# Seven block products in the last unit's third pair, routing steps spread anew, expert weights asked for later

## The chip, the cores and the metric

The kernel runs on one core of a Trainium2 chip. What counts is the time of one execution on the device, in microseconds (us). The engines named below are TensorE (PE, matrix products), VectorE (DVE), ScalarE (ACT), GpSimd (POOL) and SyncE (SP, which issues DMAs).

## What is computed

Three layers follow one another, for 4 batches of 576 positions and 512 features: linear attention over 8 heads; a block `u + relu(u @ w_ch1) @ w_ch2` with `u = x + U,V mixing`, hidden width 2048; and a top-1 mixture of 8 experts, hidden width 1024. The part of the reference that the change touches:

```python
    u = x + h.transpose(0, 2, 1)
    ch = np.maximum(u @ w_ch1, 0.0) @ w_ch2
    return u + ch
...
    logits = np.einsum('bsd,de->bse', x, w_gate)
    local_gate = 1.0 / (1.0 + np.exp(-np.einsum('bsd,de->bse', x, w_local).squeeze(-1)))
    for b in range(B):
        prev_e = -1
        for s in range(S):
            fresh_e = int(np.argmax(logits[b, s]))
            if s == 0 or local_gate[b, s] < 0.5:
                e = fresh_e
            else:
                e = prev_e if prev_e >= 0 else fresh_e
            prev_e = e
            ...
            h = np.maximum(x[b, s] @ w1[e], 0.0)
            out[b, s] = p[e] * (h @ w2[e])
```

All is in fp32. The kernel splits each fp32 operand into a high and a low part and does three matmuls for each product (high by high, low by high, high by low), so PE's work is three times what the reference says.

## The kernel before

**Stages.** Attention comes first. Then come 12 items of the feed-forward block: 4 units (g = 0 to 3, a quarter of the hidden width each) by 3 pairs p, where a pair is two blocks of 384 columns (TW). They are items 0 to 11, and unit 3 is items 9, 10 and 11. Then come 8 items of the experts: 4 batches by 2 units, with two blocks of 288 columns (CH), items 12 to 19. Each item has two matrices, so two phases on PE: a first matrix from x (L1168 to L1170) with a relu to h, and a second from h into y. A 2 by 2 by 2 block product takes eight block products; with sums of blocks made beforehand and afterwards it takes seven (the Strassen-Winograd scheme), which is 84 matmuls in place of 96. First matrices use seven in most items (the blocks are A11 to A22 and the sums S1 to S4 of the weights; B11 to B22 and the sums T1 to T4 of the moving side). DVE makes the sums afterwards: u adds, `t1`, `t3` and `t2` (psf<-psf,u), in this order, then the low parts of h (L1131). In the last unit, items 9 and 10 (`ZI`) use seven for the second matrix too (`z_steps`, matmuls on L1168 to L1170 as well); item 11 uses the plain form (`mm2`, L1494 to L1496). For that plain form the fourth weight block V3 is parked in DRAM (`park`, `wd`) and fetched again (`w_back`).

**Order of work.** The program is recorded by hand: generators for the item's steps, and threads for weights ("w") and x ("x"), are advanced side by side, and a model of each engine's time (`free`) decides when a thread goes on. Each engine then works through its own list in order. After each step of an item (13 to 16 of them) `side` runs.

**Routing.** From item 10 on `side` starts `route(b)` for batch b (item 10 + b), eleven stages which choose the expert that the batch uses. `PLANS[b]` gives for each stage the step, counted from that item's step 0 with 16 to an item, at which it is recorded. The stages are: the gate's 16 matmuls, their transposes with a maximum (`lg`, `r_sh`), three stages of small DVE instructions that end with the rows `tr`, five transposes of `tr` on PE (L1605) with six ACT copies (L1609), a scan over the positions on DVE (L1612), a count (L1616), a product (L1619), DMAs, and the maximum over the experts (`r_ix`) that gives the index of the expert.

**Weights of the experts.** `w_moe` loads a unit's weights by DMA on SP into half buffers (`halfraw`: 4 halves of `raw`, and rows as long as more than 5 are free, up to 7), and for each block ACT makes the high part (L379) and DVE subtracts it for the low part (L373). For seven block products `w_seven` also makes the weights' sums. The weights of the first batch are asked for at step 7 of item 11.

Of the kernel before, what the change touches and what calls it, by code (L numbers as in the profile page):

```python
# [7 lines left out]
F32 = mybir.dt.float32  # L8
# [8 lines left out]
B, H, S, D, F = 4, 8, 576, 64, 128  # L17
# [17 lines left out]
ZU, ZI = (3,), (9, 10)  # L35
# [8 lines left out]
def model(ctx, tc, kq, vx, wphi, ident, up, vp, wff, wg, wmoe1, wmoe2, rconst, outT):  # L44
    nc = tc.nc
# [126 lines left out]
    touched = {}  # L172
    threads = []
    force = [False]
# [144 lines left out]
    wd = dram.tile([4, 8, 128, 512], F32, name="wd")  # L319
# [15 lines left out]
    pieces = {}  # L335
# [75 lines left out]
    def park(u, s, f):  # L411
        nc.sync.dma_start(out=wd[u.g, PIECES.index(s)], in_=f[:, :512])
        there.add((u, s))
# [91 lines left out]
    def w_seven(u, get, free_, eng, p, due, flat=False, pre=""):  # L505
# [24 lines left out]
        else:  # L530
# [6 lines left out]
            if pre:  # L537
                while touched.get(id(a21), 0.0) > free["PE"] + 0.3 and not force[0]:
                    yield "wait"
                park(u, ZV["A21"], a21)  # L540
                touched[id(a21)] = max(transfer(256), touched.get(id(a21), 0.0) + 3.0)
# [32 lines left out]
    def w_back(u, due):  # L574

        yield from parked(u, (ZV["A21"],))
        s = ZV["A21"]
        yield from w_end(u, s, pieces.pop((u, s)), nc.gpsimd, rows)

    halfraw, loading = [], []  # L580

    def w_moe(u, due):
# [10 lines left out]
        while len(halfraw) < 7 and len(loading) == 1 and len(rows) > 5:  # L593
            halfraw.append(rows.pop()[:, :512])
# [749 lines left out]
    def z_item(i):  # L1344
        return i in ZI
# [30 lines left out]
    def z_steps(i):  # L1376
# [10 lines left out]
        def product(w, x, name, first):  # L1387
# [10 lines left out]
            if i == ZI[-1] and w[0] == "S":  # L1398
                wfree.append(u.w.pop("z" + w))
# [249 lines left out]
    PLANS = ((3,10,11,12,12,13,17,18,19,20,22), (8, 10, 11, 12, 12, 14, 18, 20, 21, 22, 25), (2, 5, 7, 9, 11, 14, 16, 18, 20, 22, 25), (2, 5, 7, 9, 11, 14, 16, 18, 20, 22, 25))  # L1649
    PLAN_COST = ((0.0, 0.8, 1.2), (1.4, 0.0, 0.6), (0.6, 0.0, 0.0), (0.7, 0.0, 0.0), (0.6, 0.0, 0.0), (0.0, 2.3, 0.6), (1.4, 0.0, 0.0), (0.75, 0.0, 0.0), (0.75, 0.0, 0.0), (0.0, 0.0, 0.0), (1.2, 0.0, 0.0))  # L1650

    def side(i, step, steps):
# [42 lines left out]
        if i == ZI[-1] and step == 8:  # L1695
            spawn("w", i, w_back(u, i))
        if i == nf - 1 and step == 7:
            spawn("w", last[units[4]], w_moe(units[4], last[units[4]]))
# [4 lines left out]
    def work():  # L1703

        for i in range(n):
# [10 lines left out]
            if z_item(i):  # L1716
                for _ in z_steps(i):
                    side(i, step, steps)
                    step += 1
                    yield  # L1720
                wanted[0] -= 4
                if i == ZI[-1]:
                    u = items[i][0]
                    for s in ("A11", "A12", "A22"):
                        u.w[ZV[s]] = u.w.pop("z" + s)
                        u.done.add(ZV[s])
                continue
# [217 lines left out]
```

## Time and profile before

| | |
|---|---|
| median of 3 runs | 759.8 us (759.16 to 761.56) |
| profiled execution | 760.08 us |
| its span | 758.2 us |
| PE busy | 745.3 us (98%) |
| DVE busy | 637.7 us (84%) |
| ACT busy | 351.7 us (46%) |
| POOL busy | 72.5 us (10%) |

The profile's page and the views of the trace come from the one profiled execution. A row's start is in us from the start of the span. A timeline's row gives the start, the length, the engine, line and instruction, the tiles (out<-in), how many instructions it stands for, and in brackets the idle time before it with what ended it. An instruction's length includes the time until its result is written, so the next can start on the same engine a little before its end; the spacing of starts tells what it costs its engine.

### The profile page before, as it was taken

What the parts mean: (1) busy time and instruction counts of PE and PEld (TensorE: products, weight loads), DVE (VectorE), ACT (ScalarE), POOL (GpSimd) and SP (SyncE); (2) the same over time, 40 slices, a digit from 0 to 9 for tenths busy, and PEclk for the clock granted to TensorE, in tenths of its full rate; (3) what the DMA queues carried; (4) which work ended last, traced back from release to release, by engine and by line L of the source; (5) the groups of instructions that cost most, each with busy time, mean ns of one, the idle gap of its engine ahead of it and who ended that gap; (6) DMA issues with size and microseconds to landing.
All of it is one profiled execution on the core that took longest, in us unless ns stands there. A gap on an engine that the chain in (4) does not pass through costs nothing. (4 is left out here: it accounts for less than half of the span.)

```text
span 758.2 us, 18724 instructions
## 1 busy us (share of the span) xinstructions
PE 745.3 (98%) x7656; PEld 724.1 (96%) x7656; DVE 637.7 (84%) x1277; ACT 351.7 (46%) x769; POOL 72.5 (10%) x116
## 2 busy tenths in 40 slices
PE   7999999999999999999999999999999999999997
PEld 5899898999999999999999999999999999999997
DVE  6889899777569999999799485879877899999975
ACT  5677777665152343313223133343545455555450
POOL 0212233111110000100101001010000000000000
PEclk9999999999999999999999999999999999999999
DMA  6444755324468897950469004482363144243421
GB/s 203 151 132 126 260 183 189 111 80 154 181 242 328 302 332 284 346 171 29 166 241 339 18 1 157 153 287 84 114 210 101 32 125 143 68 136 108 136 69 65
DMA packets 52728, 124.27 MB, mean 164 GB/s; under 512 B 5472, under 2 KB 29152, under 8 KB 52640
## 3 DMA queue, kind: packets, MB, share of 16 engines
q1 hardware_dynamic: 43024, 87.20, 34.1%
q0 software_dynamic: 6160, 32.39, 12.3%
q10 hardware_dynamic: 3456, 3.46, 1.3%
q8 instruction: 61, 1.00, 0.5%
q14 instruction: 27, 0.22, 0.1%
HBM read 88.81 MB, written 34.23 MB: 162 GB/s over the span
## 5 line engine op out<-in xcount | busy, mean ns | idle before, releaser
L1169 PE MATMUL psf<-x,w 128*128 128x384 f32 (+1 forms) x576 | 184.1, 320 | 0.6 <-POOL x L76 0.6
L1168 PE MATMUL psf<-x,w 128*128 128x384 f32 (+1 forms) x576 | 184.4, 320 | 0.0
L1170 PE MATMUL psf<-x,w 128*128 128x384 f32 (+1 forms) x576 | 183.9, 319 | 0.0
L1494 PE MATMUL psf<-h,w 128*128 128x384 f32 (+1 forms) x576 | 182.8, 317 | 0.0
L1495 PE MATMUL psf<-h,w 128*128 128x384 f32 (+1 forms) x576 | 182.3, 316 | 0.0
L1496 PE MATMUL psf<-h,w 128*128 128x384 f32 (+1 forms) x576 | 182.2, 316 | 0.0
L1146 ACT ACTIVATE h<-psf 128x384 fp32r<-128x384 f32 (+1 forms) x144 | 62.9, 457 | 106.7 <-DVE psf L1129 77.7
L1168 PEld LDWEIGHTS psf<-x,w 128*128 128x128 f32 x576 | 108.3, 188 | 1.4 <-issue 1.4
L1169 PEld LDWEIGHTS psf<-x,w 128*128 128x128 f32 x576 | 108.2, 188 | 1.0 <-POOL x L76 0.9
L1494 PEld LDWEIGHTS psf<-h,w 128*128 128x128 f32 x576 | 108.1, 188 | 0.5 <-issue 0.5
L1170 PEld LDWEIGHTS psf<-x,w 128*128 128x128 f32 x576 | 108.2, 188 | 0.0
L1495 PEld LDWEIGHTS psf<-h,w 128*128 128x128 f32 x576 | 108.1, 188 | 0.0
L1496 PEld LDWEIGHTS psf<-h,w 128*128 128x128 f32 x576 | 108.1, 188 | 0.0
L1129 DVE TENSOR_TENSOR y<-psf,y 128x384 f32<-128x384 f32 (+1 forms) x132 | 69.1, 530 | 24.9 <-PE psf L1496 21.3
L1131 DVE SCALAR_TENSOR_TENSOR h<-psf,h 128x384 fp32r<-128x384 f32 (+1 forms) x148 | 69.0, 508 | 21.5 <-ACT h L1146 20.9
L379 ACT CAST w<-row 128x512 fp32r<-128x512 f32 x79 | 46.7, 620 | 53.9 <-DVE row L373 31.8
L373 DVE TENSOR_TENSOR w<-row,w 128x512 fp32r<-128x512 f32 x79 | 52.9, 687 | 10.6 <-ACT w L379 10.6
L857 DVE TENSOR_REDUCE mx<-pj 128x6 f32<-128x768 f32 (+2 forms) x49 | 45.8, 935 | 6.8 <-PE pj L854 6.7
L858 DVE TENSOR_TENSOR pg<-pj,mx 128x768 f32<-128x768 f32 (+2 forms) x49 | 46.1, 941 | 2.5
L887 PE MATMUL kv<-vt,ek 128*64 128x65 f32 (+1 forms) x1152 | 47.1, 230 | 0.8 <-DMA vt<-in_vx 0.8
L756 POOL DMA_DIRECT2D x<-xd x41 | 22.0, 535 | 269.4 <-PE psf L1170 232.5
L1129 DVE TENSOR_TENSOR u<-psf,p 128x384 f32<-128x384 f32 (+1 forms) x64 | 32.4, 513 | 15.3 <-PE psf L1170 14.2
(136 smaller groups left out, 1126.7 us busy)
## 6 DMA issues: line engine op xcount, KB each, us to landing
x<-xd POOLq DMA_DIRECT2D x41, 768.0 KB, 6.9
raw<-in_wff SPq DMA_DIRECT2D x32, 512.0 KB, 3.6
xd<-x SPq DMA_DIRECT2D x21, 768.0 KB, 4.9
raw<-in_wmoe SPq DMA_DIRECT2D x35, 256.0 KB, 3.4
kq<-in_kq SPq DMA_DIRECT2D x14, 576.0 KB, 4.5
row<-in_wmoe SPq DMA_DIRECT2D x29, 256.0 KB, 4.0
vt<-in_vx SPq DMA_DIRECT2D x16, 325.0 KB, 3.0
ud<-y SPq DMA_DIRECT2D x4, 1152.0 KB, 6.6
```

What stands on the lines that cost most here:

```text
L373: eng.tensor_tensor(out=out, in0=a, in1=b, op=op)
L379: nc.scalar.copy(out=w[:, 0], in_=f[:, :512])
L887: nc.tensor.matmul(out[c], lhsT=e[:, half, i, c], rhs=rhs, start=(tl == 0 and half == 0), stop=(tl == 8 and half == 1), skip_group_check=True)
L1129: nc.vector.tensor_tensor(**kw)
L1131: nc.vector.scalar_tensor_tensor(op1=op1, **kw)
L1146: hat[t, f] = act(lambda: nc.scalar.activation(out=hhi, in_=src, func=ACTF.Relu), n_, ready)
L1168: nc.tensor.matmul(ps, lhsT=w[:, 0, c], rhs=x[:, 0, k, :n_], start=(first and k == 0), stop=False, skip_group_check=True)
L1169: nc.tensor.matmul(ps, lhsT=w[:, 0, c], rhs=x[:, 1, k, :n_], start=False, stop=False, skip_group_check=True)
L1170: nc.tensor.matmul(ps, lhsT=w[:, 1, c], rhs=x[:, 0, k, :n_], start=False, stop=(stop and k == 1), skip_group_check=True)
L1494: nc.tensor.matmul(ps, lhsT=wh, rhs=hhi, start=(k == 0), stop=False)
L1495: nc.tensor.matmul(ps, lhsT=wl, rhs=hhi, start=False, stop=False)
L1496: nc.tensor.matmul(ps, lhsT=wh, rhs=hlo, start=False, stop=(k == 3))
```

## The change

Item 11 uses seven block products for its second matrix, as items 9 and 10 do (`z_item` is true for all of unit 3). So parking V3, `w_back` and renaming the weights for `mm2` go, and `wd` has two units in place of four. The weights of the first batch's expert are asked for at step 9 of item 11, not 7. `PLANS[0]` and `PLANS[1]` have other steps. The `w_moe` loop that gives rows to the half buffers tests `len(loading) <= 1` where it tested `== 1`; the list has been appended to just before, so it has one entry at the first call either way. As item 11 holds rows for its second matrix, five half buffers come about, not seven (raw's four and one row).

```diff
-ZU, ZI = (3,), (9, 10)
+ZU = (3,)
...
-    wd = dram.tile([4, 8, 128, 512], F32, name="wd")
+    wd = dram.tile([2, 8, 128, 512], F32, name="wd")
...
-            if pre:
-                while touched.get(id(a21), 0.0) > free["PE"] + 0.3 and not force[0]:
-                    yield "wait"
-                park(u, ZV["A21"], a21)
-                touched[id(a21)] = max(transfer(256), touched.get(id(a21), 0.0) + 3.0)
...
-    def w_back(u, due):
-
-        yield from parked(u, (ZV["A21"],))
-        s = ZV["A21"]
-        yield from w_end(u, s, pieces.pop((u, s)), nc.gpsimd, rows)
-
...
-        while len(halfraw) < 7 and len(loading) == 1 and len(rows) > 5:
+        while len(halfraw) < 7 and len(loading) <= 1 and len(rows) > 5:
...
     def z_item(i):
-        return i in ZI
+        return items[i][0].kind == "ffn" and items[i][0].g in ZU
...
-            if i == ZI[-1] and w[0] == "S":
+            if last[u] == i:
                 wfree.append(u.w.pop("z" + w))
...
-    PLANS = ((3,10,11,12,12,13,17,18,19,20,22), (8, 10, 11, 12, 12, 14, 18, 20, 21, 22, 25), (2, 5, 7, 9, 11, 14, 16, 18, 20, 22, 25), (2, 5, 7, 9, 11, 14, 16, 18, 20, 22, 25))
+    PLANS = ((3, 10, 12, 16, 17, 18, 19, 20, 20, 21, 24), (10, 17, 18, 19, 20, 21, 22, 24, 26, 27, 30), (2, 5, 7, 9, 11, 14, 16, 18, 20, 22, 25), (2, 5, 7, 9, 11, 14, 16, 18, 20, 22, 25))
...
-        if i == ZI[-1] and step == 8:
-            spawn("w", i, w_back(u, i))
-        if i == nf - 1 and step == 7:
+        if i == nf - 1 and step == 9:
             spawn("w", last[units[4]], w_moe(units[4], last[units[4]]))
...
-                if i == ZI[-1]:
-                    u = items[i][0]
-                    for s in ("A11", "A12", "A22"):
-                        u.w[ZV[s]] = u.w.pop("z" + s)
-                        u.done.add(ZV[s])
                 continue
```

What the instructions' order makes of it is shown at three places. In the new program the same lines have smaller numbers by 11 (L1129 is L1118, L1612 is L1601, L1494 is L1483).

On DVE in the first phase of item 11, before, from the end of batch 0's third small stage (`tr`) to the first t1 add (psf<-psf,u; x2 is two in a row, u are the sums of products, p is a copy of the first product, y the running result):

```order
L1129 TENSOR_TENSOR y<-psf,y 128x384 x2
L373 TENSOR_TENSOR w_100<-row_90,w_100 128x512
L1129 TENSOR_TENSOR u_3712<-psf,u_3711 128x384 x2
L1129 TENSOR_TENSOR y<-y,u_3711 128x2x384
L1129 TENSOR_TENSOR y<-y,u_3712 128x2x384 x2
L1612 SCALAR_TENSOR_TENSOR row_89<-row_85,row_89 8x576
L1129 TENSOR_TENSOR u_3711<-psf,p_3710 128x384 x2
L1616 TENSOR_REDUCE r_cnt<-row_89 8x1
L1619 TENSOR_TENSOR row_84<-row_84,row_89 8x576
L1129 TENSOR_TENSOR u_3712<-psf,p_3710 128x384
L1129 TENSOR_TENSOR psf<-psf,u_3712 128x384
```

The same place after:

```order
L1583 TENSOR_TENSOR tr<-r_ex,r_sm 128x5x8
L1118 TENSOR_TENSOR u_3711<-psf,p_3710 128x384 x2
L1118 TENSOR_TENSOR y<-y,u_3712 128x2x384 x2
L76 TENSOR_TENSOR x_106<-y,x_106 128x2x288
L1601 SCALAR_TENSOR_TENSOR row_90<-row_89,row_90 8x576
L1118 TENSOR_TENSOR u_3712<-psf,p_3710 128x384 x2
L1118 TENSOR_TENSOR h_96<-row_84,h_96 128x768
L1605 TENSOR_REDUCE r_cnt<-row_90 8x1
L1608 TENSOR_TENSOR row_85<-row_85,row_90 8x576
L1118 TENSOR_TENSOR psf<-psf,u_3712 128x384 x2
L1118 TENSOR_TENSOR psf<-u_3712,psf 128x384 x2
```

The second u adds, the low part of h_96, and the pair of t1 adds stand behind the scan now, and behind an x subtract (L76); two more x subtracts and the third and fourth of the small stages, which stood in item 10, are recorded just ahead of this piece.

On DVE in front of and in item 12, before, where batch 1's `tr` is done in item 11 and the next rows are weights (w<-row, w<-raw), y adds, and low parts of h:

```order
L1129 TENSOR_TENSOR y<-psf,y 128x384
L373 TENSOR_TENSOR w_3693<-row_84,w_3693 128x512
L373 TENSOR_TENSOR w_104<-row_89,w_104 128x512
L373 TENSOR_TENSOR w_99<-row_85,w_99 128x512
L1129 TENSOR_TENSOR y<-psf,y 128x384
L373 TENSOR_TENSOR w_102<-raw_92,w_102 128x512
L1129 TENSOR_TENSOR y<-psf,y 128x384
L1131 SCALAR_TENSOR_TENSOR h_97<-psf,h_97 128x288 x2
L76 TENSOR_TENSOR x_3703<-y,x_3703 128x2x288
L1131 SCALAR_TENSOR_TENSOR h_95<-psf,h_95 128x288
```

After, the last small stage of batch 1 (L1580 to L1583, which makes `tr`) stands among the low parts of item 12's h:

```order
L1578 COPY tr<-r_fr 128x5x8
L373 TENSOR_TENSOR w_104<-row_87,w_104 128x512
L1120 SCALAR_TENSOR_TENSOR h_97<-psf,h_97 128x288
L1580 TENSOR_REDUCE r_sm<-r_ex 128x5
L1581 TENSOR_SCALAR r_sm<-r_sm 128x5
L1582 RECIPROCAL r_sm<-r_sm 128x5
L1583 TENSOR_TENSOR tr<-r_ex,r_sm 128x5x8
L373 TENSOR_TENSOR w_102<-raw_92,w_102 128x512
L1120 SCALAR_TENSOR_TENSOR h_97<-psf,h_97 128x288
L1549 TENSOR_REDUCE lg<-psf 128x27
```

The five transposes on PE that read `tr` have moved with it from the end of item 11 to the middle of item 12's first phase.

On DVE around the t2 adds of item 14 (batch 1, first unit; h are the relu's results, psf_7609 and psf_7616 the last product's banks), before:

```order
L1131 SCALAR_TENSOR_TENSOR h3_97<-psf_7592,h3_97 128x288
L1131 SCALAR_TENSOR_TENSOR h3_97<-psf_7599,h3_97 128x288
L1129 TENSOR_TENSOR psf_7609<-psf_7609,u2_3711 128x288
L1129 TENSOR_TENSOR psf_7616<-psf_7616,u2_3711 128x288
L373 TENSOR_TENSOR raw1_93<-raw1_93,row5_89 128x512
L1131 SCALAR_TENSOR_TENSOR h2_96<-psf_7609,h2_96 128x288
L1131 SCALAR_TENSOR_TENSOR h2_96<-psf_7616,h2_96 128x288
L373 TENSOR_TENSOR w12_3697<-row6_90,w12_3697 128x512
L373 TENSOR_TENSOR w3_101<-raw1_93,w3_101 128x512
```

After, where the last product's banks are psf_7608 and psf_7615:

```order
L1120 SCALAR_TENSOR_TENSOR h2_96<-psf_7588,h2_96 128x288
L1120 SCALAR_TENSOR_TENSOR h2_96<-psf_7595,h2_96 128x288
L1118 TENSOR_TENSOR psf_7608<-psf_7608,u2_3711 128x288
L1118 TENSOR_TENSOR psf_7615<-psf_7615,u2_3711 128x288
L373 TENSOR_TENSOR w3_101<-raw1_93,w3_101 128x512
L373 TENSOR_TENSOR w9_3694<-raw0_92,w9_3694 128x512
L373 TENSOR_TENSOR w12_3697<-raw1_93,w12_3697 128x512
L373 TENSOR_TENSOR row5_89<-raw0_92,row3_87 128x512
L1120 SCALAR_TENSOR_TENSOR h0_94<-psf_7608,h0_94 128x288
```

Behind the two t2 adds stands at once the subtract for the low part of w3_101. PE at the end of the first phase of item 14 and the first matmuls of its second, before:

```order
L1169 MATMUL psf_7616<-x4_3702,w13_3698 128x288
L1170 MATMUL psf_7616<-x4_3702,w13_3698 128x288
L1494 MATMUL psf_7712<-h1_95,w5_103 128x288
L1495 MATMUL psf_7712<-h1_95,w5_103 128x288
L1496 MATMUL psf_7712<-h1_95,w5_103 128x288
L1494 MATMUL psf_7712<-h1_95,w5_103 128x288
L1495 MATMUL psf_7712<-h1_95,w5_103 128x288
L1496 MATMUL psf_7712<-h1_95,w5_103 128x288
L1494 MATMUL psf_7712<-h0_94,w0_98 128x288
```

After:

```order
L1158 MATMUL psf_7615<-x4_3702,w2_100 128x288
L1159 MATMUL psf_7615<-x4_3702,w2_100 128x288
L1483 MATMUL psf_7710<-h1_95,w10_3695 128x288
L1484 MATMUL psf_7710<-h1_95,w10_3695 128x288
L1485 MATMUL psf_7710<-h1_95,w10_3695 128x288
L1483 MATMUL psf_7710<-h1_95,w10_3695 128x288
L1484 MATMUL psf_7710<-h1_95,w10_3695 128x288
L1485 MATMUL psf_7710<-h1_95,w10_3695 128x288
L1483 MATMUL psf_7710<-h3_97,w3_101 128x288
```

The weight that the seventh to twelfth matmul of the second matrix read was w0_98 and is w3_101. In item 16 the same stands: the subtract for w4_102 follows the two t2 adds.

## Rows read from the trace of the kernel before

**Rows 1.** The page: busy us, share of the span and instructions of PE.

```profile
PE 745.3 (98%) x7656; PEld 724.1 (96%) x7656; DVE 637.7 (84%) x1277; ACT 351.7 (46%) x769; POOL 72.5 (10%) x116
```

**Rows 2.** Waits of PE, 455 to 600 us: us in total, times, longest.

```profile
PE psf L1168 <- DVE y L1129: 0.3, 1, 0.3
```

**Rows 3.** Windows: length, busy us (instructions) by engine, clock, DMA share, GB/s.

```profile
460.17:474.73 14.56, 14.56 (x86) 14.56 (x85) 8.95 (x16) 5.13 (x9) 3.18 (x6) 1.00 0.70 229
474.73:489.48 14.75, 14.75 (x85) 14.55 (x85) 13.92 (x26) 5.25 (x9) 0.53 (x1) 1.00 0.40 149
...
610.83:621.94 11.11, 11.11 (x86) 11.11 (x85) 10.92 (x24) 6.07 (x14) 0.99 (x2) 1.00 0.59 174
...
658.27:669.38 11.11, 11.11 (x86) 11.11 (x85) 10.66 (x24) 5.22 (x13) 0.00 (x0) 1.00 0.63 192
```

**Rows 4.** Timeline of PE, item 10's end: start, length, instruction, idle before and releaser.

```profile
518.43 0.34 PE L1170 MATMUL psf<-h,w 128*128 128x384 f32 x1
519.03 0.41 PE L1168 MATMUL psf<-h,w 128*128 128x384 f32 x1 [0.26 <-DVE y L1129]
519.28 0.34 PE L1169 MATMUL psf<-h,w 128*128 128x384 f32 x1
```

**Rows 5.** DVE groups in item 10's first phase: busy us, mean ns, idle before.

```profile
L1129 DVE TENSOR_TENSOR u<-psf,p 128x384 f32<-128x384 f32 x4 | 2.2, 558 | 3.5 <-PE psf L1170 3.5
...
L1129 DVE TENSOR_TENSOR psf<-psf,u 128x384 f32<-128x384 f32 x2 | 1.1, 566 | 1.4 <-PE psf L1170 1.4
```

**Rows 6.** Timeline of DVE, first phase of item 11.

```profile
520.12 0.18 DVE L1591 TENSOR_REDUCE r_sm<-r_ex 128x5 f32<-128x40 f32 x1
...
520.88 1.01 DVE L1129 TENSOR_TENSOR y<-psf,y 128x384 f32<-128x384 f32 x2
...
522.41 1.01 DVE L1129 TENSOR_TENSOR u<-psf,u 128x384 f32<-128x384 f32 x2
523.34 2.69 DVE L1129 TENSOR_TENSOR y<-y,u 128x768 f32<-128x768 f32 x3
525.94 1.34 DVE L1612 TENSOR_TENSOR_SCAN row<-row,row 8x576 f32<-8x576 f32 x1
527.21 0.98 DVE L1129 TENSOR_TENSOR u<-psf,p 128x384 f32<-128x384 f32 x2
528.12 0.73 DVE L1616 TENSOR_REDUCE r_cnt<-row 8x1 f32<-8x576 f32 x1
528.78 0.73 DVE L1619 TENSOR_TENSOR row<-row,row 8x576 f32<-8x576 f32 x1
...
532.81 0.75 DVE L76 TENSOR_TENSOR x<-y,x 128x576 fp32r<-128x576 f32 x1
```

**Rows 7.** Timeline of ScalarE (ACT), start of item 11.

```profile
521.61 2.45 ACT L1609 COPY row<-psf 8x256 f32<-8x256 f32 x6 [5.01 <-PE psf L1605]
```

**Rows 8.** Timeline of DVE, item 10: the second half of t1.

```profile
501.40 0.57 DVE L1129 TENSOR_TENSOR psf<-psf,u 128x384 f32<-128x384 f32 x1 [0.47 <-PE psf L1170]
```

**Rows 9.** Timeline of ACT, item 10: what follows that t1.

```profile
502.00 0.49 ACT L1238 ACTIVATE row<-psf 128x384 f32<-128x384 f32 x1 [0.55 <-DVE psf L1129]
502.52 0.84 ACT L1363 CAST h<-row 128x768 fp32r<-128x768 f32 x1
```

**Rows 10.** Timeline of DVE, item 12: two weight subtracts.

```profile
564.18 1.30 DVE L373 TENSOR_TENSOR w<-raw,w 128x512 fp32r<-128x512 f32 x2
```

**Rows 11.** Timeline of DVE, around the start of item 14's second phase.

```profile
620.64 2.34 DVE L1131 SCALAR_TENSOR_TENSOR h<-psf,h 128x288 fp32r<-128x288 f32 x6
622.89 0.82 DVE L1129 TENSOR_TENSOR psf<-psf,u 128x288 f32<-128x288 f32 x2
623.62 0.69 DVE L373 TENSOR_TENSOR raw<-raw,row 128x512 f32<-128x512 f32 x1
```

**Rows 12.** Timeline of PE: the eighth matmul of item 14's second phase.

```profile
622.86 0.29 PE L1495 MATMUL psf<-h,w 128*128 128x288 f32 x1
```

**Rows 13.** Timeline of DVE: the t2 adds of item 16.

```profile
669.60 0.82 DVE L1129 TENSOR_TENSOR psf<-psf,u 128x288 f32<-128x288 f32 x2
```

## Prediction

> **What bounds the kernel now.** I read the page's busy times first. TensorE (PE) is busy 745.3 us of the 758.2 us span, 98% [rows 1]. The granted clock is 1.00, the 2.4 GHz level, in every stretch I read. Next came the waits of PE in the 145 us around the change: one, of 0.3 us [rows 2]. Last came the windows by phase, where PE is busy for all of nearly every phase [rows 3]. So two things alone move the end here: matmuls taken away from PE, and waits given to it. A PE wait anywhere after 480 us moves the end by its full length, since no idle time is left behind it to take it up.
>
> The profiled execution took 760.08 us: 758.2 of span and 1.88 outside. The median of the runs is 759.8, so I sum against 760.08 and take 0.28 off at the end. I call "same" what lies within 0.3% of 759.8, that is 757.5 to 762.1; a measurement of this kernel tells no finer.
>
> **What the change takes off PE.** The second matrix of item 11 (unit 3, third pair) goes from 96 matmuls to 84. A phase of 84 such matmuls takes 14.56 us, so 0.1733 each [rows 3]. Twelve matmuls by 0.1733 is **-2.08 us**. The one PE wait sits in front of the last product of item 10: matmuls stand at 518.43 and 519.03 where 0.17 would do, so 0.43 us [rows 4]. It waits for an add to y that stands behind 0.8 us of routing work on VectorE (DVE). In the new order that add comes ahead of the routing, so **-0.43 us**. The parking and fetching of V3 goes too (two DMAs, a cast, a subtract); its DVE share is one 0.60 us subtract, and as DVE still has idle time in item 10 (below) I price it at nothing on PE. The smaller DRAM buffer and the `<= 1` in `w_moe` cost nothing: the list has one entry there either way. All told PE has 2.5 us less to do; if nothing else happened the run would take 757.6, or **757.3** on the median's scale.
>
> **Item 11's first matrix, new order.** With seven products for the second matrix, DVE must make the combinations of h between the two matrices, and PE's last product of the first matrix (S4) is held until `t1` (the add psf<-psf,u) has read its bank. In item 10, which already works so, DVE came to these adds early: it idled 3.5 us ahead of the u adds and 1.4 us ahead of t1, each time for PE [rows 5]. In item 11 the plan of batch 0's route now puts its stages 3 and 4, its scan, its count and its product into the same stretch, and three x subtracts come ahead of the scan too. Prices from starts that follow one another [rows 6]: route stage 0.76 (520.12 to 520.88), x subtract 0.66 (its 0.75 less the 0.09 by which such starts overlap), wide add to y 0.87 (2.60 for three), pair of u adds 0.93, scan 1.27, count 0.66; the product at the end is like the count. Item 11 starts at about 520.8 (without the wait and without the five transposes, which now come after its third product). DVE is free at 521.0 and does one u add 0.47, two stages 1.5, three x subtracts 2.0, three wide adds 2.6 and the first u pair 0.9: 528.5. The scan then waits for ScalarE's six route copies, 2.45 us [rows 7], which can begin only when the transposes are through at about 527.4: 529.8. Scan 1.27, second u pair 0.9, the low half of B22 0.87 (as a wide add), count and product 1.3: t1 starts at 534.15, not at 531. S4 is due at 533.8 (520.8 + six products of 2.08 + 0.5 for the transposes) and gets its bank at 534.9: **+1.1 us** (0 to 1.3; the lower end if DVE gets through 1 us sooner).
>
> The second matrix then needs the low half of B11 at its second matmul. After the second t1 add the relu follows by 0.60, the cast by another 0.52, and the cast lasts 0.84 [rows 8, 9]: 1.96, then 0.95 for the low half. With t1 at 534.6 that is 537.5, where PE would want it at 537.1: 0.5 us with the restart. T1's low half stands behind more adds in the same queue and costs about as much again. Items 9 and 10 show 0.19 of this already (14.75 for 84 matmuls where 14.56 would do) [rows 3], and since I have no shorter chain, I take **+0.9** (0 to 1.1).
>
> One place for the Trainium skill. Adds with an operand in PSUM follow each other at 0.46 here (522.41 to 523.34 for two) [rows 6]. "Perfetto Trace Analysis", section "Optimizing Scalar/DVE Operations", gives DVE a fixed overhead of about 60 ns on SBUF and 125 ns on PSUM. By it each of these adds would stand 65 ns longer in the queue; the rows show no such difference between u adds and half of a wide SBUF add beyond 0.03, so the rows' spacing is what I sum, and by the page's figure t1 would come about 0.5 us later (eight such adds, an estimate).
>
> **Item 12.** Route 1's transposes move from the end of item 11 into item 12, directly behind the stage that makes `tr`. That work is equal, but three restarts behind short transposes cost about 0.1 each, as the start at 519.03 (0.25 to the next, where 0.17 is the rule) [rows 4]: **+0.3**. In front of the transposes DVE must do, after item 11's tail of three wide adds (2.6) and two u adds (0.9), ten pieces: four stages of 0.8, five low halves of 0.38 (2.34 for six), one weight subtract of 0.65 (1.30 for two) [rows 10, 11]. From 555.3, where the last product of item 11 gives its result, that is 3.5 + 3.2 + 1.9 + 0.65 = 564.6 if it never waits. It does wait for relus, since ScalarE has two weight casts and an exponential in front of one of them: 1.7 us at most, 566.3 to 567. PE wants `tr` at 565.5. I take **+1.1** (0 to 1.6).
>
> **Items 14 and 16.** Here the weights matter. Half buffers for expert weights fall from seven to five, because item 11 still holds rows when they are dealt out, and the load is asked for two steps later. The order shows the effect twice: the low half of the second weight that the second matrix needs is now subtracted directly behind the two t2 adds, and PE reads it in its eighth matmul. In the trace those adds start at 622.89 as a pair, 0.73 in all, and the phase at 621.94; the eighth matmul is at 622.86 [rows 3, 11, 12]. With the subtract (0.69, rows 11) behind them it is ready at 624.35, with 0.05 to hand on; the matmul stalls by about 1.5. The t2 adds are late by six products with h (2.34) in front of them; if DVE came on time they would end at about 622.5 and the stall would be 0.4. I take **+1.1** (0.4 to 1.9). Item 16: the adds start at 669.60, the phase at 669.38 [rows 3, 13]; 669.60 + 0.73 + 0.65 + 0.05 = 671.0 against 670.3 (0.92 into the phase, as in item 14), **+0.8** (0.4 to 1.2). In the order of before the two weights that this phase reads first are subtracted some 25 DVE instructions ahead of the t2 adds, so none of this can be seen in the trace.
>
> **Sum.** -2.08 - 0.43 + 1.1 + 0.9 + 0.3 + 1.1 + 1.1 + 0.8 = +2.8; 760.08 + 2.8 - 0.28 = **762.6 us**. All waits at their upper ends (1.3, 1.1, 0.3, 1.6, 1.9, 1.2) give 764.7; at their lower ends (0.8 in items 14 and 16, 0.3 in item 12) 758.4.
>
> **Rivals.**
> *All waits hidden, faster.* DVE is busy only 84% over the span. If ScalarE's route copies come earlier than I think, so that the scan doesn't wait 1.2 us, t1 is on time, S4 and both second-matrix products start without a gap, and the tail into item 12 is short enough for `tr` to be made in time. With t2 on time too, only the 2.5 us remain: 757.3. It decides at t1: at or before 533.0 in item 11. For it: item 10 does the same work with 6 us of DVE idle. Against: item 11 has over 6 us of extra DVE work in that stretch. The Trainium skill leans this way: "Perfetto Trace Analysis", section "Identifying the Most-Contended Engine", says to optimize the engine with the highest occupancy first. That is PE, and by that rule the saved matmuls come through; the trace agrees on which engine it is, but averages over the stretch where DVE is the tighter one.
> *Items 11 and 12 as summed, weights on time in 14 and 16:* +0.9, 760.7. For it: the two phases are 90 us behind the change, and DVE may reach the t2 adds early there.
> *Items 14 and 16 as summed, items 11 and 12 nearly clean:* -2.5 + 0.3 + 1.9, 759.5.
> *The change doesn't save matmuls:* excluded by the order, which has 12 fewer on PE.
>
> **How the numbers follow.** Waits in both places, 760.8 to 764.7, of which most is above 762.1: 0.55. Weights on time: 0.16. Items 11 and 12 clean: 0.15. All hidden: 0.14. Of the first case I put 0.09 within 762.1, so slower 0.46, same 0.40 (0.09 + 0.16 + 0.15), faster 0.14. The range has to reach to the hidden case, as it and the two middle cases hold 0.45: 757.2 to 764.7.
>
> **What will show it.** Right or wrong, item 11's second phase has 84 matmuls of 384 columns and no add of y waits ahead of 519. A PE wait of about 1 us ahead of S4 of item 11 and two of 0.5 in the next two products show the DVE queue; a wait ahead of the transposes of item 12 shows the plan; a wait of about 1 us at the eighth matmul of the second phases of items 14 and 16, released by a weight subtract, shows the weights. I am wrong if t1 in item 11 starts within 0.3 us of PE's fifth product, or if these two weight subtracts end ahead of the phase's start.

## The result, and the profile after

The changed kernel takes 763.89 us (median of 7 runs, 762.77 to 765.13) where the kernel before takes 759.68 us in the same rounds. The ratio is 1.0055, with a 95% interval of 1.0046 to 1.0064: slower by 4.2 us. The forecast was 762.6 us and slower.

The profiled execution of the changed kernel took 763.36 us, with a span of 761.6. The page's first line, to be held against [rows 1], and PE's waits from 455 us to 600 us and from 600 us to the end (us in total, times, longest), the first of them against [rows 2]:

```profile
PE 745.3 (98%) x7644; PEld 722.2 (95%) x7644; DVE 647.9 (85%) x1290; ACT 354.7 (47%) x775; POOL 71.9 (9%) x116
```
```profile
PE psf L1594 <- DVE tr L1583: 1.1, 1, 1.1
PE psf L1158 <- DVE h L1118: 0.7, 2, 0.4
PE psf L1157 <- DVE psf L1118: 0.5, 1, 0.5
```
```profile
PE psf L1484 <- DVE w L373: 2.2, 2, 1.3
PE psf L1157 <- DVE u L1118: 0.7, 1, 0.7
PE psf L1159 <- DVE w L373: 0.4, 1, 0.4
```

PE has 12 matmuls fewer (7644 for 7656). Its busy time is the same 745.3 us even so, in part because the first matmul after a wait is longer (0.40 us below, where [rows 12] has 0.29). Every PE wait that is new is ended by DVE, which does 10.2 us more work (647.9 for 637.7). One wait of 0.3 us has become eight, of 5.6 us in all. Where these stand shows in the windows by phase (length, busy us and instructions of PE, PEld, DVE, ACT and POOL, clock, DMA share, GB/s). Before, the second phase of item 10, both of item 11, the first of item 12, and the second phases of items 14 and 16 (the first phases of these two are in [rows 3]):

```profile
505.36:521.65 16.29, 16.03 (x95) 15.45 (x95) 15.85 (x43) 6.05 (x12) 0.00 (x0) 1.00 0.20 75
521.65:536.30 14.65, 14.65 (x88) 14.65 (x86) 14.24 (x29) 7.13 (x16) 1.02 (x2) 1.00 0.29 110
536.30:555.32 19.02, 19.02 (x124) 17.98 (x123) 15.56 (x44) 7.30 (x16) 0.00 (x0) 1.00 0.47 153
555.32:569.92 14.60, 14.60 (x121) 13.74 (x119) 9.73 (x21) 9.74 (x23) 1.00 (x2) 1.00 0.67 220
...
621.94:634.58 12.64, 12.64 (x98) 12.64 (x97) 12.50 (x30) 6.75 (x16) 0.00 (x0) 1.00 0.26 79
...
669.38:682.03 12.65, 12.65 (x99) 12.65 (x97) 12.40 (x24) 8.22 (x18) 0.00 (x0) 1.00 0.35 109
```

The same phases after, with the first phases of items 14 and 16:

```profile
504.54:519.87 15.33, 15.33 (x91) 15.09 (x90) 15.15 (x35) 6.63 (x12) 0.00 (x0) 1.00 0.13 51
519.87:535.72 15.85, 15.37 (x90) 14.99 (x90) 14.22 (x30) 7.37 (x15) 1.01 (x2) 1.00 0.27 102
535.72:552.84 17.12, 16.43 (x101) 14.85 (x101) 16.98 (x37) 8.92 (x17) 0.00 (x0) 1.00 0.25 80
552.84:569.68 16.84, 15.78 (x128) 14.72 (x128) 13.48 (x42) 8.59 (x22) 0.00 (x0) 1.00 0.61 206
...
610.54:622.58 12.04, 11.35 (x86) 11.12 (x85) 11.41 (x25) 6.97 (x16) 0.98 (x2) 1.00 0.51 157
622.58:636.84 14.26, 12.91 (x99) 12.68 (x98) 12.02 (x29) 6.69 (x15) 0.00 (x0) 1.00 0.31 100
...
660.53:672.30 11.77, 11.33 (x87) 11.10 (x85) 11.67 (x26) 6.82 (x15) 0.00 (x0) 1.00 0.49 161
672.30:686.11 13.81, 12.91 (x98) 12.68 (x97) 13.15 (x25) 8.20 (x18) 0.00 (x0) 1.00 0.38 119
```

| stretch | before | after | difference |
|---|---|---|---|
| item 10, second phase | 16.29 | 15.33 | -0.96 (five transposes moved on, 0.4 of wait gone) |
| item 11, first phase | 14.65 | 15.85 | +1.20 (the five transposes, a wait) |
| item 11, second phase | 19.02 | 17.12 | -1.90 (12 matmuls and ten transposes less, two waits more) |
| item 12, first phase | 14.60 | 16.84 | +2.24 (ten transposes, a wait) |
| item 14, both phases | 23.75 | 26.30 | +2.55 |
| item 16, both phases | 23.76 | 25.58 | +1.82 |

Up to the end of item 12's first phase the sum is +0.58; the saved matmuls are more than paid back there. Items 14 and 16, which begin 58 and 108 us after item 11's second matrix has ended, cost another 4.37. Items 13, 15, 17, 18 and the first phase of item 19 have their old lengths to within 0.1 us. The six differences come to 4.95. The two profiled executions differ by 3.28 only, since the one of after was 0.8 us quicker ahead of item 9 (459.37 for 460.17) and 0.7 behind item 19's first phase, in work that is the same; the medians differ by 4.2.

In item 11 the chain that holds the last product of the first matrix (S4) is seen in three rows: the scan waits for ScalarE's copies, t1 comes behind it, and PE waits for t1.

```profile
528.52 1.35 DVE L1601 TENSOR_TENSOR_SCAN row<-row,row 8x576 f32<-8x576 f32 x1 [0.74 <-ACT row L1598]
...
532.93 1.01 DVE L1118 TENSOR_TENSOR psf<-psf,u 128x384 f32<-128x384 f32 x2
```
```profile
533.54 0.44 PE L1157 MATMUL psf<-x,w 128*128 128x384 f32 x1 [0.48 <-DVE psf L1118]
```

In item 14 the picture is the one of [rows 11, 12]. The DVE timeline there, then PE's (start, length, instruction, idle time before it with its releaser):

```profile
621.29 2.34 DVE L1120 SCALAR_TENSOR_TENSOR h<-psf,h 128x288 fp32r<-128x288 f32 x6
623.54 0.82 DVE L1118 TENSOR_TENSOR psf<-psf,u 128x288 f32<-128x288 f32 x2
624.27 1.89 DVE L373 TENSOR_TENSOR w<-raw,w 128x512 fp32r<-128x512 f32 x3
```
```profile
625.01 0.40 PE L1484 MATMUL psf<-h,w 128*128 128x288 f32 x1 [1.34 <-DVE w L373]
```

ScalarE casts the high parts of three weights from 614.52 to 616.19. By their order these are the three whose subtracts start at 624.27, so neither the load nor the cast is late:

```profile
614.52 1.67 ACT L379 CAST w<-raw 128x512 fp32r<-128x512 f32 x3
```

### The profile page after: what moved, and what is told of

Its sections match the earlier page's. It is cut to its first block, busy times and chain, and to the rows that moved or that the text cites. A ratio compares the mean times of both kernels' runs of the same rounds, so it can differ in the third digit from the quotient of the medians.

```text
span 761.6 us, 18711 instructions
## 1 busy us (share of the span) xinstructions
PE 745.3 (98%) x7644; PEld 722.2 (95%) x7644; DVE 647.9 (85%) x1290; ACT 354.7 (47%) x775; POOL 71.9 (9%) x116
## 5 line engine op out<-in xcount | busy, mean ns | idle before, releaser
L1159 PE MATMUL psf<-x,w 128*128 128x384 f32 (+1 forms) x576 | 183.9, 319 | 0.4 <-DVE w L373 0.4
L1484 PE MATMUL psf<-h,w 128*128 128x384 f32 (+1 forms) x544 | 171.7, 316 | 2.2 <-DVE w L373 2.2
L1483 PE MATMUL psf<-h,w 128*128 128x384 f32 (+1 forms) x544 | 171.9, 316 | 0.0
L1485 PE MATMUL psf<-h,w 128*128 128x384 f32 (+1 forms) x544 | 171.5, 315 | 0.0
L1159 PEld LDWEIGHTS psf<-x,w 128*128 128x128 f32 x576 | 108.2, 188 | 0.7 <-DVE w L373 0.7
L1484 PEld LDWEIGHTS psf<-h,w 128*128 128x128 f32 x544 | 102.1, 188 | 2.7 <-DVE w L373 2.7
L1135 ACT ACTIVATE h<-psf 128x384 fp32r<-128x384 f32 (+1 forms) x136 | 58.7, 454 | 97.8 <-DVE psf L1118 63.7
L1483 PEld LDWEIGHTS psf<-h,w 128*128 128x128 f32 x544 | 102.1, 188 | 0.1
L1485 PEld LDWEIGHTS psf<-h,w 128*128 128x128 f32 x544 | 102.1, 188 | 0.0
L1118 DVE TENSOR_TENSOR y<-psf,y 128x384 f32<-128x384 f32 (+1 forms) x134 | 69.4, 527 | 24.7 <-PE psf L1485 21.1
L1120 DVE SCALAR_TENSOR_TENSOR h<-psf,h 128x384 fp32r<-128x384 f32 (+1 forms) x142 | 65.8, 505 | 16.9 <-ACT h L1135 16.1
L379 ACT CAST w<-row 128x512 fp32r<-128x512 f32 x62 | 37.0, 619 | 45.8 <-DVE row L373 19.9
L373 DVE TENSOR_TENSOR w<-row,w 128x512 fp32r<-128x512 f32 x62 | 41.8, 685 | 10.8 <-ACT w L379 10.8
L379 ACT CAST w<-raw 128x512 fp32r<-128x512 f32 x60 | 35.9, 622 | 21.7 <-DVE raw L373 14.3
```

The source lines that it names most:

```text
L379: nc.scalar.copy(out=w[:, 0], in_=f[:, :512])
L1118: nc.vector.tensor_tensor(**kw)
L1120: nc.vector.scalar_tensor_tensor(op1=op1, **kw)
L1135: hat[t, f] = act(lambda: nc.scalar.activation(out=hhi, in_=src, func=ACTF.Relu), n_, ready)
L1159: nc.tensor.matmul(ps, lhsT=w[:, 1, c], rhs=x[:, 0, k, :n_], start=False, stop=(stop and k == 1), skip_group_check=True)
L1483: nc.tensor.matmul(ps, lhsT=wh, rhs=hhi, start=(k == 0), stop=False)
```

## The experiments

Theories at the start: (A) the weights are late in items 14 and 16 because five half buffers came about in place of seven; (B) they are late because DVE's queue is full of the second matrix's adds. Each run below is a kernel with the edit that is shown or named; times are medians, and the ratio is to the kernel before in the same round.

**Five half buffers in the kernel before.**

```diff
-        while len(halfraw) < 7 and len(loading) == 1 and len(rows) > 5:
+        while len(halfraw) < 5 and len(loading) == 1 and len(rows) > 5:
```

> The kernel before with five half buffers for the expert weights in place of seven, and nothing else. Theory A (five half buffers are what makes the weights late in items 14 and 16): waits of 1 to 1.6 us for a weight subtract in the second phases of items 14 and 16, so 762 to 764 us. Theory B (DVE's queue is full only because of the adds of the second matrix in item 11; the half buffers alone don't matter): no PE wait beyond the 0.3 us of before, 759.7 us, within 0.5.

Measured: 760.56 us, ratio 1.0007 (0.9997 to 1.0016). Its PE waits from 455 us on:

```profile
PE psf L1168 <- DVE u L1129: 0.4, 1, 0.4
PE psf L1168 <- DVE y L1129: 0.3, 1, 0.3
```

No wait for a weight. Theory A falls as a cause by itself: five half buffers don't make a weight late in the order of before. Five buffers alone bring one wait of 0.4 us, for the u adds of item 14, which is also one of the waits of the changed kernel.

**Nine half buffers in the changed kernel.**

```diff
-        while len(halfraw) < 7 and len(loading) <= 1 and len(rows) > 5:
+        while len(halfraw) < 7 and len(rows) > 3:
```

> The changed kernel, with rows given to the expert weights at every call while more than three are free, so that nine half buffers come about in place of five. Theory A and B alike: the low halves of the weights come ahead of the t2 adds in items 14 and 16, the four waits there (4.4 us from item 14's start to item 17's, against the kernel before) go, and the waits of items 11 and 12 stay: 759 to 760 us. A rival, that DVE lacks the time for these subtracts whatever the buffers: the waits move to other weights and the time stays at 763 to 764 us.

Measured: 765.62 us, ratio 1.007 (1.0053 to 1.0086). A miss in the time, though the first half of the expectation came true: the waits for weights are gone. PE's waits from 455 us on:

```profile
PE psf L1547 <- ACT row L1541: 3.9, 1, 3.9
...
```

The three lines left out are those of the changed kernel up to 600 us, unchanged. So more buffers are one way to have these weights on time; the number of buffers counts together with the order. (Of the 64 loads of expert weights 33 go to rows here, 12 in the changed kernel.)

The rows that went to the buffers are missed by the routing: in item 13 ScalarE's copy of the gate's result (L1541) waits until DVE's product of another batch's route has read the row that it is to fill, and PE's transposes wait 3.9 us for that copy.

```profile
601.93 0.70 ACT L1541 COPY row<-psf 128x288 f32<-128x288 f32 x2 [2.46 <-DVE row L1608]
```

The wait cost more than its 3.9 us. The granted clock is 0.50 (the 1.2 GHz level) in each us from 601 to 607, and 15 matmuls behind the transposes start 0.24 us apart, where 0.13 is usual at the 2.4 GHz level: 1.6 us more, an estimate from these starts. In the phases of the changed kernel shown above, where the longest wait is 1.34 us, the granted clock is 1.00 throughout.

**The second matrix alone**, with the plans and the asking of before.

```diff
-    PLANS = ((3, 10, 12, 16, 17, 18, 19, 20, 20, 21, 24), (10, 17, 18, 19, 20, 21, 22, 24, 26, 27, 30), ...
+    PLANS = ((3,10,11,12,12,13,17,18,19,20,22), (8, 10, 11, 12, 12, 14, 18, 20, 21, 22, 25), ...
...
-        if i == nf - 1 and step == 9:
+        if i == nf - 1 and step == 7:
```

> Seven block products for item 11's second matrix alone: the plans of before, weights asked for at step 7, five half buffers. If the new plans and the later asking make the late weights of items 14 and 16, these are gone here and about 4 us with them: 759 to 761 us, with new waits of 1 to 2 us at the start of item 12, where the low halves of the first two weights stand behind item 11's last adds. If the second matrix's adds alone make them, 763 to 765 us. If the plans of before suited the second matrix as well, 757.5 us.

Measured: 769.69 us, ratio 1.0122 (1.0105 to 1.0139). Its PE waits from 536 us to 580 us:

```profile
PE psf L1159 <- DVE w L373: 5.8, 1, 5.8
PE psf L1540 <- DVE row L1120: 1.1, 1, 1.1
...
```

The new wait is where it was expected, but 5.8 us long and not 1 to 2. Items 14 and 16 have no late weights, as expected. With the old plans the second matrix costs 1.2%; the new plans and the later asking mend a little over half of it (0.55% is left). DVE's list at item 12's start shows why the wait is so long: all of batch 1's small stages, two x subtracts and item 11's last adds stand ahead of the first weight subtracts, at 559.91.

```profile
557.30 2.68 DVE L1118 TENSOR_TENSOR y<-y,u 128x768 f32<-128x768 f32 x3
559.91 1.28 DVE L373 TENSOR_TENSOR w<-raw,w 128x512 fp32r<-128x512 f32 x2
```

Here too the clock fell: it is 0.50 from 558 to 563 us, and the matmuls from 561.05 to 562.97 start 0.24 us apart. PE's first rows behind the wait:

```profile
560.64 0.61 PE L1159 MATMUL psf<-x,w 128*128 128x288 f32 x1 [5.79 <-DVE w L373]
561.05 0.44 PE L1157 MATMUL psf<-x,w 128*128 128x288 f32 x1
561.29 0.44 PE L1158 MATMUL psf<-x,w 128*128 128x288 f32 x1
```

**The plans, one at a time.** Batch 1's new plan alone (batch 0's old one, asking at step 7):

> The changed kernel with batch 0's old plan and the weights asked for at step 7 again, so that of the plans only batch 1's is new. If batch 0's spread and the later asking carry the repair of item 12 (5.8 us of waiting for a weight without any of the new plans): 768 to 770 us. If batch 1's spread carries it: 763 to 764.5 us, with the late weights in items 14 and 16 as they are, which would also clear the later asking of them.

Measured: 765.43 us, ratio 1.0066 (1.005 to 1.0083), 0.9 us above the second range. The 5.8 us of waiting in item 12 are gone. In its profile PE waits for weights in the second phases of items 14 and 16 as in the changed kernel (2.2 us for two), and 1.5 us for `tr` in item 12.

Batch 0's new plan and the later asking alone:

> The other half: batch 0's new plan and asking at step 9, batch 1's old plan. If batch 1's plan is what keeps the weights of item 12 from being late: waits of 3 to 5 us for weights in item 12 and 766 to 768 us. If batch 0's plan carries it: 763 to 764.5 us.

Measured: 774.36 us, ratio 1.0188 (1.017 to 1.0206). PE waits 5.2 us for weights on L1159 (4.7 of them between 540 and 580 us), 2.0 us in item 11's gate and 1.8 us for a weight in item 16's second phase. The waits in item 12 are as expected, but the time is 6 us above the range. Two things more are in it. The granted clock is 0.50 from 561 to 566 us, behind a wait of 3.1 us. And no row was given to the half buffers when they were dealt out, so that this run has four of them: all 64 loads go to `raw`, where the changed kernel sends 12 to rows.

```profile
raw<-in_wmoe SPq DMA_DIRECT2D x64, 256.0 KB, 2.9
```

So this run doesn't show batch 0's plan by itself. What the plans do is read from the two runs that differ in batch 1's plan alone, both asking at step 7 with 12 loads to rows. With the old plan (769.69 us) a weight is 5.8 us late in item 12 and none in items 14 and 16; with the new one (765.43 us) it is the other way round. So batch 1's plan is the repair, and it brings the late weights of items 14 and 16 with it, whether the weights are asked for at step 7 or 9. It is not the only thing that can: item 16 has a late weight in the run with four half buffers too, with batch 1's old plan.

**The route's product on GpSimd.**

```diff
-        nc.vector.tensor_tensor(out=tp, in0=tp, in1=ta, op=ALU.mult)
+        nc.gpsimd.tensor_tensor(out=tp, in0=tp, in1=ta, op=ALU.mult)
```

> The changed kernel with the product of each route (8 x 576) on GpSimd in place of DVE: 0.67 us less in DVE's queue in items 11, 12, 13 and 14, at the place just ahead of t1 or the h products. If PE waits for the length of DVE's queue, the 0.5 us wait ahead of S4 in item 11 goes, the two waits of 0.3 to 0.4 us behind it shrink, and the waits for weights in items 14 and 16 get up to 0.7 us shorter: 761.5 to 762.5 us. If the waits are for something else (DMA, ScalarE), 763.9 us as it is.

Measured: 764.41 us, ratio 1.0051 (1.0034 to 1.0068): no difference from the changed kernel. It decides nothing about the length of the queue, because the 0.67 us did not come free. While GpSimd does its product, DVE's subtract beside it takes 1.54 us; the same instruction takes 0.96 in the changed kernel. The GpSimd and DVE rows of this run, and the DVE row of the changed kernel:

```profile
531.00 1.43 POOL L1608 TENSOR_TENSOR row<-row,row 8x576 f32<-8x576 f32 x1 [28.66 <-DVE row L1601]
```
```profile
531.71 1.54 DVE L1118 TENSOR_TENSOR h<-row,h 128x768 fp32r<-128x768 f32 x1
```
```profile
530.73 0.96 DVE L1118 TENSOR_TENSOR h<-row,h 128x768 fp32r<-128x768 f32 x1
```

**Weight subtracts further ahead** in expert items: the changed kernel with other figures in the table that says how far ahead of PE the recorder may put them.

```diff
-    MOE_SLACK = (2.0,0.4,1.5,0.3,0.0,0.0,0.0, 1.0, 2.5, 2.5, 2.5, 2.5, 2.5, 2.5, 2.0)
+    MOE_SLACK = (2.0,0.4,1.5,1.0,1.0,1.0,2.0, 2.5, 2.5, 2.5, 2.5, 2.5, 2.5, 2.5, 2.0)
```

> The changed kernel with one table of the recorder altered: in steps 3 to 7 of an expert item it may put a weight subtract 0.7 to 2 us further ahead of PE. DVE does the same work; the subtracts of w3_101 and of item 16's weight now stand ahead of the h products and the t2 adds. Theory C (the waits in items 14 and 16 come from the place of these subtracts in DVE's queue, since their high parts are ready some 8 us earlier): the second-phase waits there (1.6 and 1.2 us with their restarts) and item 16's first-phase wait go, 760 to 761 us. Theory D (DVE has no time left in these items, so what is put ahead makes something else late): 763 to 764 us, with waits for h or t2 in place of those for the weights.

Measured: 762.94 us, ratio 1.0037 (1.0023 to 1.0051). The waits for weights are gone, and DVE does the same work; that the place of the subtracts in its queue makes them late (theory C) holds for them. In the changed kernel one subtract of a weight stands at 617.03 and three behind the t2 adds, from 624.27. Now three stand together from 618.01, ahead of the h products, and the fourth at 624.63, still ahead of the t2 adds (625.97); all four are in time:

```profile
618.01 1.88 DVE L373 TENSOR_TENSOR w<-raw,w 128x512 fp32r<-128x512 f32 x3
```

Windows of item 14 (both phases), of item 16 (both) and of item 18's first phase:

```profile
611.53:624.04 12.51, 11.51 (x86) 11.04 (x84) 11.88 (x25) 6.91 (x16) 0.99 (x2) 1.00 0.60 173
624.04:636.79 12.75, 12.75 (x97) 12.75 (x97) 12.54 (x31) 7.21 (x18) 0.00 (x0) 1.00 0.33 102
660.49:671.55 11.06, 11.06 (x87) 11.06 (x85) 10.67 (x24) 5.12 (x12) 0.00 (x0) 1.00 0.64 191
671.55:684.19 12.64, 12.64 (x99) 12.64 (x97) 12.64 (x26) 7.37 (x17) 0.00 (x0) 1.00 0.38 122
707.89:720.04 12.15, 11.22 (x86) 10.98 (x84) 11.14 (x27) 5.74 (x13) 0.00 (x0) 1.00 0.69 215
```

Items 14 and 16 are 2.9 us shorter than in the changed kernel (48.96 for 51.88), but item 18's first phase, ended by a wait for h, is about 1.0 longer than item 16's. That is a part of theory D: DVE is so nearly full there that a wait comes back at another place. The medians gave back some 1.4 us (by the two ratios, whose intervals just overlap), so the time lies between what theories C and D had forecast.

**Less DVE work, same order.** The last wide adds of items 10 and 11 over 32 columns.

```diff
-            dve(2 * TW, 0.0, src, out=ys(r, t), in0=ys(r, t), in1=as_x(src), op=op)
+            c = 32 if i > nf - 3 else TW
+            dve(2 * TW, 0.0, src, out=ys(r, t)[:, :, :c], in0=ys(r, t)[:, :, :c], in1=as_x(src)[:, :, :c], op=op)
```

> The changed kernel with the three wide adds to y that end the second matrix of items 10 and 11 done over 32 columns in place of 384 (so a part of the sums is left out of y): 2.2 us less DVE work in item 11's first phase, ahead of the scan, and 2.2 us less at the start of item 12. The order is the same. If the wait ahead of S4 is DVE's work before the scan, it goes (0.5 us and the two behind it); if it is the chain from ScalarE's route copies through the scan, it stays. The wait of 1.1 us ahead of item 12's transposes goes. If the late weights of items 14 and 16 are a backlog carried from item 12, these waits shrink by about 2 us: 758 to 760 us; if they are their place in the queue, they stay: 762 to 763 us.

The sums that it leaves out change which experts positions choose, and a further part of the program runs for them at the end; its total (2331 us) says nothing here, so only the trace up to 700 us is read. PE's waits there, and DVE's scan in item 11:

```profile
PE psf L1485 <- DVE w L373: 2.2, 2, 1.3
...
PE psf L1159 <- DVE w L373: 0.6, 1, 0.6
PE psf L1595 <- DVE tr L1584: 0.5, 1, 0.5
PE psf L1157 <- DVE psf L1118: 0.5, 1, 0.5
```
```profile
529.58 1.35 DVE L1602 TENSOR_TENSOR_SCAN row<-row,row 8x576 f32<-8x576 f32 x1 [2.74 <-ACT row L1599]
```

Three answers. The wait ahead of S4 stays at 0.5 us: DVE is 2 us earlier, and the scan waits these 2 us longer for ScalarE's route copies (2.74 us of idle time, 0.74 in the changed kernel), so the chain is transposes, copies, scan, t1. The wait for `tr` falls by 0.6 of its 1.1 us, and was expected to go; the rest of it is not the tail of item 11. The late weights of items 14 and 16 stay at 2.2 us: they are no backlog carried from item 12.

**Two new spreads**, chosen by the order: the places found above are mended, the second matrix stays.

```diff
+    MOE_SLACK = (2.0, 0.4, 0.5, 1.0, 0.5, 1.0, 2.0, 2.5, 2.5, 3.5, 2.0, 2.5, 2.5, 3.0, 2.0)
...
+        while len(halfraw) < 7 and len(rows) > 5:
...
+    PLANS = ((3, 10, 11, 15, 16, 17, 18, 19, 21, 21, 23), (11, 18, 18, 19, 20, 22, 23, 25, 27, 27, 30), ...
...
+        if i == nf - 1 and step == 10:
```

> The changed kernel with the routing stages of the first two batches spread once more (batch 0: 3, 10, 11, 15, 16, 17, 18, 19, 21, 21, 23; batch 1: 11, 18, 18, 19, 20, 22, 23, 25, 27, 27, 30), the weights asked for at step 10 with rows dealt at every call while more than five are free, and the weight subtracts of expert items let further ahead as in the run with the altered table. In its order item 11's scan stands ahead of the u adds with its product behind t1, batch 1's transposes one step behind their stage, and the weights of items 14 and 16 ahead of the t2 adds. If place in DVE's queue is the whole loss, the waits of items 11, 12, 14 and 16 fall to under 1 us in all and of the 2.5 us taken off PE 1 to 2 are left: 757.5 to 759 us, at or just under the kernel before. If DVE has no room for the second matrix's adds, other waits take their place: 760 to 763 us.

Measured: 759.43 us, ratio 0.9989 (0.998 to 0.9998), 0.4 us above the first range. PE's waits from 455 us to the end hold one line again, and item 11's second phase and item 12's first have lost their waits:

```profile
PE psf L1157 <- DVE y L1118: 0.3, 1, 0.3
```
```profile
536.58:552.68 16.10, 16.10 (x101) 14.91 (x101) 15.96 (x35) 9.70 (x18) 0.00 (x0) 1.00 0.32 100
552.68:568.29 15.61, 15.61 (x128) 14.71 (x128) 13.39 (x42) 7.23 (x19) 0.00 (x0) 1.00 0.63 217
```

It is faster than both kernels: than the changed one by some 5 us, and than the one before by 0.8 us, which is only just clear of the noise. DVE does the same work as in the changed kernel (647.3 us for 647.9). Plans, dealing, asking and table were altered together, so what each of them gave is not shown. From item 9's start to the end of item 12's first phase it takes 107.85 us (460.44 to 568.29), and the kernel before 109.75 (460.17 to 569.92): 1.9 us of the 2.5 are there. Behind that point small delays, too short for the list of waits, take more than half of it back (item 14's second phase is 13.15 for 12.64, item 18's first 11.45).

The second spread has another table as well:

```diff
+    MOE_SLACK = (2.0, 0.4, 1.5, 1.0, 1.0, 1.0, 2.0, 3.0, 2.5, 2.5, 2.5, 2.5, 2.5, 2.0, 2.3)
```

> Another spread for the same end (batch 0: 3, 10, 12, 15, 16, 17, 18, 19, 19, 21, 24; batch 1: 9, 17, 19, 19, 19, 22, 23, 25, 27, 28, 31), rows dealt at the first call only, asking at step 10, the weight subtracts let further ahead: five half buffers as in the changed kernel. If half buffers don't matter once the places are right: 758 to 759.5 us, as in the run beside it. If they do, a wait for weights of 1 us or more comes back in items 12 to 16: 760 to 762 us.

Measured: 760.75 us, ratio 1.0013 (1.0002 to 1.0025): neither half of the expectation came true, since the time is that of the second and the waits for weights stayed away. Waits of 0.6 us for u in item 14, of 0.4 for h in item 11, of 0.3 for h; none for a weight, with five half buffers. It has the wait for u that the kernel before shows with five buffers. It shows that weights can be on time with five, and not what the buffers cost, since the plans and the table differ too.

## Why the prediction came out as it did

It was right in direction and range (757.2 to 764.7), right in the mechanism (PE waits for what stands late in DVE's queue) and 1.3 us short in size. By place it was less even than the total says: items 10 to 12 were summed to +0.9 and came to +0.58, items 14 and 16 to +1.9 and came to +4.37. The shortfall in the stretches is 2.2 us (4.95 for 2.8); in the medians it is 1.4, and what gives the rest back there is not shown. Point by point, by the terms of its sum:

- *12 matmuls, -2.08, and the wait at 519, -0.43:* right. The second phase of item 10 is 0.96 shorter, of which the five transposes are some 0.55.
- *S4's bank, +1.1:* the mechanism is right, the size is half: 0.48 us of idle time. The scan waited for ScalarE as summed (0.74 where I had 1.2), and t1 started 13.1 us after the item (532.93 and 519.87), not 13.35. The run with narrow adds shows that the work ahead of the scan isn't on the chain: the sum had that right, as it goes by the copies (529.8, not 528.5), but its lower end hadn't, which lets the wait go when DVE gets through 1 us sooner. DVE was 2 us sooner, and the wait stayed.
- *Second matrix of item 11, +0.9:* the phase takes 17.12; without 16 gate matmuls (1.2 busy, with their restarts 1.3) and 14.56 that leaves 1.25, of which 0.19 was in [rows 3]: +1.06. Right.
- *Item 12, +0.3 and +1.1:* the wait for `tr` was 1.06. The phase is 2.24 longer, so 1.18 is left for ten transposes, which cost 1.08 in item 11 before (19.02 less 96 matmuls, 16.64, and 1.3 for the gate). So of the 0.3 for restarts about 0.1 is seen, and the term is near 1.2 in all, for 1.4.
- *Items 14 and 16, second phases, +1.1 and +0.8:* measured +1.62 and +1.16. The sums from the rows had given 1.5 and 0.7. For item 14 I took less, by an average with a lower end that nothing in the trace supported: DVE did not come sooner, the t2 adds start 0.96 us into the phase (623.54) as they did before (622.89).
- *Items 14 and 16, first phases:* no term. They cost 0.93 and 0.66: the u adds behind the scan in item 14, a weight of the second product in item 16. This is the step that failed by omission. I priced the phases where the order shows a subtract just ahead of the matmul that reads it, and not the first phases of the same items, where DVE was as full (10.92 and 10.66 of 11.11 us in [rows 3]).

Its reason for the late weights was half wrong. "Half buffers fall from seven to five" doesn't make them late by itself (run with five buffers in the kernel before, no wait for a weight; more of them in the changed kernel do take the waits away), and asking later isn't needed for it (batch 1's plan with the early asking has them too). What the prediction said at the end of that paragraph, that the place in DVE's queue counts, is what the altered table showed.

Of the rivals, *items 11 and 12 nearly clean* would have needed the copies to be earlier; *weights on time* is what the altered table gave, at 762.9 us and not 760.7, since a wait came back in item 18 and the first phase of item 14 stayed. *All waits hidden* (757.3) wasn't reached by any run; the best spread came to 759.4. Its sign was badly chosen: t1 did start before 533.0 (532.93), since the item began 0.9 us earlier than summed, and PE waited for it all the same. And the rule of the Trainium skill that the engine with the highest occupancy is the one to relieve first ("Perfetto Trace Analysis", section "Identifying the Most-Contended Engine") was not enough here. PE is that engine here, also by a measure that the section prefers for TensorE, the weight loads' busy share (96% in [rows 1]). But it was relieved of 2.08 us by giving DVE 10.2 us more, in a stretch where DVE was busy for 14.24 of 14.65 us before the change (item 11's first phase) and for 16.98 of 17.12 after it (its second). With another order, 0.8 us of the 2.5 came through.

What stays open: why the chain in item 12 still makes `tr` late by 0.5 us with the tail of item 11 gone. The relu that DVE waits for is the suspect, by one idle time of 1.64 us, which is as long in the run with narrow adds; no run takes it away.

```profile
560.82 0.46 DVE L1120 SCALAR_TENSOR_TENSOR h<-psf,h 128x288 fp32r<-128x288 f32 x1 [1.64 <-ACT h L1135]
```

Open too are which of the small delays behind item 12 in the best spread could be had back, and whether seven half buffers in the changed kernel would have been enough.

## What to carry to other kernels

Where an engine at 98% is fed by one at 84%, look at the second one in the stretch that is changed, and not over the span: trading 2 us of matmuls for 10 us of adds lost 4.2 us here in one order of DVE's work and gained 0.8 in another, with the same work. In a queue that works in order, an instruction's place decides and not only how much work there is: letting two of three late subtracts in item 14 start by 619.2 in place of 624.27, and their like in item 16, gave back 2.9 us in two items with no work less. A run with a long wait of PE is not to be compared by the length of its waits alone, since the clock can fall behind it (0.50 after waits of 3.1, 3.9 and 5.8 us here). When a plan's table is altered, price every phase in which the order has changed, also those far behind the edit, and the phases just ahead of the ones that stand out.

## What the runs showed that was not expected

A short GpSimd instruction cost DVE nearly what it took off it. The route's product is 0.67 us on DVE; on GpSimd it takes 1.43 (531.00 to 532.43), and the DVE subtract that overlaps it (two operands in SBUF, 768 columns) takes 1.54 where it takes 0.96 without it: its end, 533.25, is 0.82 behind the end of the GpSimd instruction, about one whole subtract (0.87 between starts) later. The u adds just ahead of it, which read PSUM, overlapped the same GpSimd instruction at their usual 0.98 for two. The product's other three runs in that kernel took 1.41 to 2.09 us, and two of them show the same beside them: a DVE instruction on 128x40 in SBUF takes 1.12 us for 0.20 (571.98), a weight subtract 1.25 for 0.67 (618.25). That agrees with what the Trainium skill says in "SBUF — State Buffer", section "Summary: rules for kernel authors": with two SBUF inputs on DVE and a GpSimd operation reading SBUF, the one that comes second is blocked until the first has finished.
